# One centred-only tile instead of two at the entry of a mixer-and-MLP kernel, w2 in one load, and a new instruction order

## The chip, the cores and the metric

The kernel runs on one core of a Trainium2 chip. The metric is the device time of one execution in microseconds. "Span" is the time from the first to the last instruction in a profiled execution; it is about 1.3 us shorter than the time of the same run.

## The reference

```python
h  = gelu(layernorm(x) @ w1)                       # x: 2048 x 512, w1: 512 x 512
# four quarters of the columns of h are shifted by +1, -1, +2, -2 tokens
x1 = x + concat(g0, g1, g2, g3) @ w2               # w2: 512 x 512
out = x1 + gelu(layernorm(x1) @ w3) @ w4           # w3: 512 x 1792, w4: 1792 x 512
```

All inputs are bf16. Tokens are worked on in 16 tiles of 128.

## The kernel before

The order of TensorE is given by hand (or by a search) in a script, and so is the order of the loads. The names used below: `ty`/`tp` is a transpose of normalised rows on TensorE, `up1` the first matmul (w1), `mix` the matmul with w2, `up2` and `down` those with w3 and w4.

Most tiles take this path at the entry: statistics, rstd, normalise to rows, transpose on TensorE into PSUM, copy back to SBUF, `up1` with the result already transposed. A tile in `NAT` takes another, and this document calls it a centred-only tile. Its rows are only centred, so its transpose needs the mean but not rstd; its first matmul makes rows, and rstd is applied as the scale of the gelu. The price is a return transpose (`th`) of the gelu's result and one more copy.

```python
GROUPS = {1: (1, 1, 1, 1, 1, 1, 2, 2, 2, 2, 2), 2: (2, 2, 4, 4, 4)}   # tiles per up1 / up2 group
STAT_ACT = (1, 6, 8, 9, 12, 21, 22, 23, 27, 28, 29)                   # statistics on ScalarE, others on VectorE
NAT = (0, 1)
SPLIT = (0,)                                                          # tile 0 works in two halves of w1
LOADS = """
x0 w1a w1b x4-5 w2b tp2 x3 w2a x6-7 w3b x8 w3a x1@act x9 x2@act x11 tp16 w4a x10 tp11 w4b tp9 x12-14 x15
"""
SCRIPT = """
warm:8 sa:0 sb:0 ty:1 ra:0 rb:0 up1:1 ty:2 th:0-1 up1:2 mix:0 ty:4 ty:3 mix:1 ...
"""
# ... cut ...
def ln(layer, t):                       # cut to its order
    # bn_stats, bn_aggr (or two passes on ScalarE) -> mean, variance
    pg.add("pool", f"rstd{q}", lambda e: e.tensor_tensor(col(rstd), var, neghalf[:], ALU.pow), ...)
    # normalise: centred-only tiles do not read rstd
# ... cut ...
def warm_pe(n):                         # dummy matmuls ahead of the first useful work
    def f(e):
        for _ in range(n):
            ins = e.matmul(o_ps[:, b, :], zeros[:, 0:P], zeros[:], start=True, stop=True)
        return ins
# ... cut ...
pg.order()                              # places all operations; pg.seq is the order that is emitted
emit(nc, es, pg)
```

Each engine executes its own list in order. `x1@act` means that the load is issued from ScalarE's queue; all other loads are issued by SyncE.

Of the kernel before, what the change touches and what calls it, by code (L numbers as in the profile page):

```python
# [6 lines left out]
P = 128  # L7
ACT_F = mybir.ActivationFunctionType
# [17 lines left out]
class Program:  # L26
# [2 lines left out]

    HOP = {"pe": 200.0, "dve": 155.0, "act": 220.0, "pool": 120.0, "sp": 70.0}  # L30
    LOOK = {"dve": 300.0, "act": 300.0}
    DUE = 252723.0
    BEGIN = {"sp": 30.0, "act": 150.0, "pe": 400.0, "dve": 150.0, "pool": 450.0}
    ENTRY = 1900.0
    COLD, RESTART = 4300.0, 800.0
# [219 lines left out]
        self.seq = out  # L255
        return out

GROUPS = {1: (1, 1, 1, 1, 1, 1, 2, 2, 2, 2, 2), 2: (2, 2, 4, 4, 4)}
NORM = {4: "act", 5: "act", 6: "act", 10: "act", 11: "pool", 12: "pool", 13: "act", 15: "act", 18: "pool", 20: "pool", 21: "pool", 22: "pool", 24: "act", 28: "act", 30: "pool"}
EVAC = {1: "both", 2: "dve", 3: "dve", 7: "both", 9: "dve", 10: "both", 11: "both", 13: "both", 16: "dve", 17: "both", 19: "both", 20: "dve", 22: "both", 23: "dve", 24: "dve", 25: "dve", 28: "dve", 31: "dve"}  # L260
STAT_ACT = (1, 6, 8, 9, 12, 21, 22, 23, 27, 28, 29)
TAIL = (256, 128, 128)
NMR = {0: "pool", 1: "pool", 3: "pool", 5: "pool", 7: "pool", 9: "pool", 10: "pool", 12: "pool", 13: "pool", 14: "pool", 17: "pool", 18: "pool", 19: "pool", 21: "pool", 22: "pool", 23: "pool", 27: "pool", 30: "pool"}
NAT = (0, 1)
SPLIT = (0,)
HEV = {2: "dve", 5: "dve", 6: "dve"}
BIAS = {}
LOADS = """
x0 w1a w1b x4-5 w2b tp2 x3 w2a x6-7 w3b x8 w3a x1@act x9 x2@act x11 tp16 w4a x10 tp11 w4b tp9 x12-14 x15
"""  # L270
SCRIPT = """
warm:8 sa:0 sb:0 ty:1 ra:0 rb:0 up1:1 ty:2 th:0-1 up1:2 mix:0 ty:4 ty:3 mix:1 up1:3 ty:5 up1:4 mix:2 up1:5
mix:3 ty:17 mix:4 up2:0 up1:6 up2:1 mix:6 down:1 mix:5 up1:7-8 mix:8 mix:7 up1:9 mix:10 down:0 down:2 mix:9
up1:10 mix:12 mix:11 up2:2 mix:13 down:3 down:6 mix:14 up2:3 mix:15 down:4-5 down:7 down:11 down:9-10 up2:4
down:8 down:12 down:14 down:13 down:15
"""

def bass_standalone__mixer_s_mlp__prompt_kernel(nc, x, w1, w2, w3, w4, out):
    B, S, D = x.shape
    F = w3.shape[1]  # L280
    assert B == 1 and D == 4 * P and S % 512 == 0 and F % (2 * P) == 0 and S >= 1024
    NT, DC, FC = S // P, D // P, F // P
# [10 lines left out]
    with ExitStack() as es:  # L293
        sb = lambda name, shape, dt: es.enter_context(nc.sbuf_tensor(name, shape, dt))
        x_sb = sb("x_sb", [P, NT, D], BF16)
        x1_sb = sb("x1_sb", [P, NT, D], BF16)
        xnT = sb("xnT", [P, DC, S], BF16)
        hT = sb("hT", [P, DC, HTW], BF16)
        h2T = sb("h2T", [P, FC, S], BF16)
        w1_sb = sb("w1_sb", [P, DC, D], BF16)  # L300
# [3 lines left out]
        ident = sb("ident", [P, P], BF16)  # L304
# [26 lines left out]
        def pair_rv(p, v):  # L331
            return [(("y", p, 0), v), (("y", p, 1), v)]
# [180 lines left out]
        def mm_up_rows(t):  # L513
            p, v = next_pair()
            k = NAT.index(t)

            def part(c0, c1):
                def f(e):
                    for dc in range(c0, c1):
                        ins = e.matmul(y_ps[:, p, 0:D], xnT[:, dc, P * t : P * (t + 1)], w1_sb[:, dc, :],  # L520
                                       start=(dc == 0), stop=(dc == DC - 1))
                    return ins

                return f

            if t in SPLIT:
                for hh in (0, 1):
                    cs = range(2 * hh, 2 * hh + 2)
                    pg.add("pe", f"rows{t}_{hh}", part(2 * hh, 2 * hh + 2),
                           reads=[(("w1", c), 0) for c in cs] + [(("xT", t, c), 1) for c in cs],  # L530
                           writes=[pair_rv(p, v)[hh]], dur=2 * 215.8)
                    if hh == 0:
                        yield
            else:
                pg.add("pe", f"rows{t}", part(0, DC),
                       reads=[(("w1", c), 0) for c in range(DC)] + [(("xT", t, c), 1) for c in range(DC)],
                       writes=pair_rv(p, v), dur=DC * 215.8)
            pg.add("act", f"gelur{t}",
                   lambda e: e.activation(hn[:, k, :], y_ps[:, p, 0:D], ACT_F.Gelu_apprx_tanh,  # L539
                                          scale=rstd[:, t : t + 1]),  # L540
                   reads=pair_rv(p, v) + [(("rstd", t), 0), (("warm",), 1)], writes=[(("hn", t), 0)], dur=50 + D * 0.833)
            yield

        def h_transpose(t, pair):
            g = group_of[1, t]
            how = HEV.get(t, "act")
            k = NAT.index(t)
            if pair:
                b, v = next_pair()
                res, dst = pair_rv(b, v), y_bf[:, b, 0:D]  # L550
            else:
                b, v = next_bank()
                res, dst = [(("o", b), v)], o_bf[:, b, 0:D]

            def f(e):
                for c in range(DC):
                    ins = e.transpose(dst[:, P * c : P * (c + 1)], hn[:, k, P * c : P * (c + 1)], ident[:])  # L557
                return ins

            pg.add("pe", f"th{t}", f, reads=[(("hn", t), 0), (("ident",), 1)], writes=res, dur=225)  # L560
            to, frm = hT[:, :, 2 + P * t : 2 + P * (t + 1)], dst.rearrange("p (c s) -> p c s", s=P)
            pg.add(how, f"evh{t}",
                   (lambda e: e.activation(to, frm, ACT_F.Copy)) if how == "act" else
                   (lambda e: e.tensor_copy(to, frm)),
                   reads=res, writes=[(("h", j, g), 0) for j in range(DC)],
                   dur=(60 + 0.82 * D) if how == "act" else (75 + 0.51 * D))


        def mm_up(layer, g):
            t0, n = groups[layer][g]  # L570
# [34 lines left out]
        def run(gen):  # L605
            for _ in gen:
                pass
# [82 lines left out]
        for step in SCRIPT.split():  # L690
            kind, n = step.split(":")
            a, _, b = n.partition("-")
            steps += [(kind, n) for n in (range(int(a), int(b or a) + 1) if kind != "warm" else [int(n)])]
        steps = [s for s in steps if s[0] not in ("th", "tz") or s[1] in NAT]
        pe_tp = {n for kind, n in steps if kind in ("tp", "ty", "sa")}
        queues = {"sp": [], "act": []}
        for i, item in enumerate(LOADS.split()):
# [10 lines left out]
        for kind, n in steps:  # L708
            if kind == "warm":
                warm_pe(n)  # L710
            elif kind in ("sa", "ra"):
                halves[kind[0], n] = pe_transpose(n, n, True) if kind == "sa" else mm_up_rows(n)
                next(halves[kind[0], n])
            elif kind in ("sb", "rb"):
                next(halves[kind[0], n])
            elif kind in ("tp", "ty"):
                run(pe_transpose(n % NT, n, kind == "ty"))
            elif kind in ("th", "tz"):
                h_transpose(n, kind == "tz")
            elif kind == "mix":  # L720
                mm_mix(n)
            elif kind == "down":
                mm_down(n)
            else:
                for _ in mm_up(int(kind[2]), n):
                    pass
# [103 lines left out]
```

## Time and profile before

| | before |
|---|---|
| median of 3 runs | 135.56 us (135.43 to 135.89) |
| span of the profiled run (the slowest of the three, 135.89 us) | 134.6 us |
| TensorE busy | 130.6 us, 97% |
| first useful matmul / last one ends | 5.01 / 132.73 us |

The page's head shows the busy times; TensorE (PE) is the limit:

```profile
span 134.6 us, 2013 instructions
PE 130.6 (97%) x780; PEld 72.7 (54%) x792; DVE 52.1 (39%) x140; ACT 58.5 (44%) x90; POOL 25.9 (19%) x59
```

The timeline of TensorE at the entry has the columns start, length, engine, line, operation, output and inputs, count, and in brackets the idle time just before and what ended it. L679 is the dummies, L482 transposes, L520 the rows of centred-only tiles, L557 their return transposes, L586 `up1`:

```profile
3.18 1.06 PE L679 MATMUL o_ps<-zeros 128*128 128x512 bf16 x2
4.03 1.01 PE L482 MATMUL y_ps<-ident,xn_buf 128*128 128x128 bf16 x8
5.01 0.59 PE L520 MATMUL y_ps<-w_sb,xnT 128*128 128x512 bf16 x2
6.04 1.47 PE L520 MATMUL y_ps<-w_sb,xnT 128*128 128x512 bf16 x6 [0.44 <-DMA w_sb<-in_w_dram]
7.35 0.39 PE L482 MATMUL y_ps<-ident,xn_buf 128*128 128x128 bf16 x4
7.57 0.39 PE L557 MATMUL o_ps<-ident,hn 128*128 128x128 bf16 x4
8.35 0.40 PE L557 MATMUL o_ps<-ident,hn 128*128 128x128 bf16 x4 [0.39 <-ACT hn L539]
```

There are two waits. The second half of w1 landed at 6.00 us and is used from 6.04, and the return transpose of tile 1 waits for its gelu until 8.35. After about 9.6 us the stream has no gap worth the name.

The table of windows gives, for the first 6 us, the length, the busy time of PE, PEld, DVE, ACT and POOL, the granted clock, the DMA share and the rate in GB/s.

```profile
0.00:6.00 6.00, 4.97 (x18) 2.06 (x18) 3.22 (x11) 3.80 (x9) 2.11 (x14) 1.00 0.77 242
```

### The profile page before, as it was taken

Reading aid. Unit: us, or ns where it says so; the run is one execution under the profiler, and the core shown is the slowest. Engines: PE = TensorE matmul, PEld = TensorE weight load, DVE = VectorE, ACT = ScalarE, POOL = GpSimd, SP = SyncE. Lnnn points to the kernel's source line nnn. Section 1 sums busy time; section 2 is a strip of 40 time slices with the busy share of each in tenths; the row PEclk is TensorE's granted clock in tenths of the full one; section 3 lists DMA queues with packets and bytes.
Section 4 is the critical chain, followed back from the end, with each engine's and each line's share of the span. In section 5 each row is a group of like instructions: output and inputs, shape, how many; then the busy total and the mean of one; then the engine's idle time right before and its main releaser. Section 6 shows DMA issues by size and latency. Waiting matters only on the chain.

```text
span 134.6 us, 2013 instructions
## 1 busy us (share of the span) xinstructions
PE 130.6 (97%) x780; PEld 72.7 (54%) x792; DVE 52.1 (39%) x140; ACT 58.5 (44%) x90; POOL 25.9 (19%) x59
## 2 busy tenths in 40 slices
PE   8889999999999999999999999999999999999994
PEld 3467688886586446444444444444444444444463
DVE  3779999403947627700053500062222200012222
ACT  6598995768484402775530366500000155520000
POOL 2533467600865301200010310010000000000000
DMA  6999398599056532111003110003111100001112
GB/s 198 298 381 380 80 294 161 98 271 271 0 117 82 118 78 78 39 39 39 5 0 78 39 39 0 0 0 85 39 39 65 52 0 0 0 5 39 39 39 78
DMA packets 21897, 12.32 MB, mean 92 GB/s; under 512 B 14464, under 2 KB 21376, under 8 KB 21888
## 3 DMA queue, kind: packets, MB, share of 16 engines
q1 hardware_dynamic: 21168, 11.80, 32.9%
q10 hardware_dynamic: 720, 0.39, 1.0%
q8 instruction: 6, 0.10, 0.3%
q14 instruction: 3, 0.02, 0.0%
HBM read 6.82 MB, written 2.10 MB: 66 GB/s over the span
## 4 chain that ended last, share of the span: by engine, by line
PE 93%; DMA 4%; issue 1%; SPq 1%; ACT 1%; DVE 0%; ACTq 0%
PE y_ps L586 45%; PE o_ps L655 36%; PE o_ps L626 10%; DMA w_sb<-in_w_dram 4%; PE y_ps L520 1%; PE y_ps L482 1%; ACT hn L539 1%; SPq L372 0%; PE o_ps L557 0%; SPq L365 0%; DVE o_sb L663 0%; ACTq L779 0%; SPq L815 0%
## 5 line engine op out<-in xcount | busy, mean ns | idle before, releaser
L586 PE MATMUL y_ps<-xnT,w_sb 128*128 128x256 bf16 (+2 forms) x421 | 62.4, 306 | 0.2
L586 PEld LDWEIGHTS y_ps<-xnT,w_sb 128*128 128x128 bf16 x424 | 39.0, 98 | 23.4 <-DVE xnT L490 0.3
L655 PE MATMUL o_ps<-w_sb,h2T 128*128 128x512 bf16 (+2 forms) x247 | 49.0, 355 | 0.3
L601 ACT ACTIVATE h2T<-y_ps 128x1024 bf16<-128x1024 f32 (+1 forms) x29 | 28.6, 994 | 42.6 <-PE y_ps L586 42.6
L655 PEld LDWEIGHTS o_ps<-w_sb,h2T 128*128 128x128 bf16 x252 | 23.6, 98 | 25.2
L663 DVE TENSOR_TENSOR o_sb<-o_ps,x_sb 128x512 bf16<-128x512 f32 (+2 forms) x18 | 11.4, 633 | 40.0 <-PE o_ps L655 39.8
L416 POOL TENSOR_TENSOR rstd<-mv,neghalf 128x1 f32<-128x1 f32 x21 | 11.7, 555 | 42.8 <-DVE mv L411 38.7
L626 PE MATMUL o_ps<-w_sb,hT 128*128 128x512 bf16 x60 | 15.2, 379 | 0.3
L409 DVE BATCH_NORM_STATS2 st<-x_sb 128x6 f32<-128x512 bf16 x21 | 14.2, 676 | 2.1 <-DMA x_sb<-in_x_dram 1.8
L637 DVE TENSOR_TENSOR x_sb<-o_ps,x_sb 128x512 bf16<-128x512 f32 x10 | 6.9, 687 | 12.7 <-PE o_ps L626 12.7
L633 DVE SCALAR_TENSOR_TENSOR x_sb<-o_ps,x_sb 128x512 bf16<-128x512 f32 x6 | 4.1, 690 | 16.8 <-PE o_ps L626 16.7
L601 ACT ACTIVATE hT<-y_ps 128x1024 bf16<-128x1024 f32 (+1 forms) x9 | 7.4, 827 | 6.3 <-PE y_ps L586 6.2
L416 POOL TENSOR_TENSOR rstd<-vpe,neghalf 128x1 f32<-128x1 f32 x11 | 6.0, 551 | 18.8 <-DVE vpe L405 18.7
L626 PEld LDWEIGHTS o_ps<-w_sb,hT 128*128 128x128 bf16 x64 | 6.0, 98 | 5.5
L437 DVE TENSOR_SCALAR xn_buf<-x_sb,mv,rstd 128x512 bf16<-128x512 bf16 x15 | 7.0, 469 | 4.9 <-POOL rstd L416 4.6
L446 ACT ACTIVATE xn_buf<-x_sb,nmr,rstd 128x512 bf16<-128x512 bf16 x8 | 6.5, 813 | 5.1 <-DVE nmr L442 3.2
L393 ACT ACTIVATE junk<-x_sb 128x512 bf16<-128x512 bf16 x11 | 6.9, 624 | 2.7 <-DVE x_sb L633 2.7
L449 POOL TENSOR_SCALAR xn_buf<-x_sb,rstd,nmr 128x512 bf16<-128x512 bf16 x7 | 5.4, 768 | 0.8 <-DVE nmr L442 0.4
L679 PE MATMUL o_ps<-zeros 128*128 128x512 bf16 x8 | 3.6, 631 | 0.6 <-POOLq L815 0.6
L411 DVE BATCH_NORM_AGGREGATE mv<-st 128x2 f32<-128x9 f32 x21 | 4.0, 191 | 0.2
L388 ACT ACTIVATE junk<-x_sb 128x512 bf16<-128x512 bf16 x5 | 3.1, 625 | 0.2 <-DMA x_sb<-in_x_dram 0.2
L482 PEld LDWEIGHTS y_ps<-ident,xn_buf 128*128 128x128 bf16 x28 | 2.3, 111 | 1.3 <-issue 0.5
(35 smaller groups left out, 30.5 us busy)
## 6 DMA issues: line engine op xcount, KB each, us to landing
w_sb<-in_w_dram SPq DMA_DIRECT2D x4, 896.0 KB, 6.8
out_dram<-o_sb SPq DMA_DIRECT2D x15, 128.0 KB, 1.7
w_sb<-in_w_dram SPq DMA_DIRECT2D x4, 256.0 KB, 5.2
x_sb<-in_x_dram SPq DMA_DIRECT2D x7, 128.0 KB, 5.2
x_sb<-in_x_dram SPq DMA_DIRECT2D x2, 256.0 KB, 5.5
xnT<-xn_buf SPq DMA_TRANSPOSE x25, 2.5
x_sb<-in_x_dram SPq DMA_DIRECT2D x1, 384.0 KB, 6.0
x_sb<-in_x_dram ACTq DMA_DIRECT2D x2, 128.0 KB, 3.0
```

Of the source, the lines that this page charges most:

```text
L393: (lambda d: (lambda e: e.activation(d, src, ACT_F.Square, accum_out=sums[:, q, 1:2])))(junk[:, b, :]),
L409: pg.add("dve", f"bnst{q}", lambda e: e.bn_stats(st9[:, q, 0:6], src), reads=rs, writes=[(("st", q), 0)], dur=605)
L416: lambda e: e.tensor_tensor(col(rstd), var, neghalf[:], ALU.pow),
L437: lambda e: e.tensor_scalar(dst, src, mv[:, q, 0:1], rstd[:, q : q + 1], ALU.subtract, ALU.mult),
L446: f = lambda e: e.activation(dst, src, ACT_F.Identity, bias=nmr[:, q : q + 1], scale=rstd[:, q : q + 1])
L449: f = lambda e: e.tensor_scalar(dst, src, rstd[:, q : q + 1], nmr[:, q : q + 1], ALU.mult, ALU.add)
L586: ins = e.matmul(y_ps[:, p, W * i : W * (i + 1)], wsb[:, dc, P * fc : P * (fc + 1)], src[:, dc, P * t0 : P * t0 + W], start=(dc == 0), sto ...
L601: (lambda d, s: (lambda e: e.activation(d, s, ACT_F.Gelu_apprx_tanh)))(dst, ysrc),
L626: ins = e.matmul(dst, hT[:, j, c0 : c0 + P], w2_sb[:, j, :], start=(j == 0), stop=(j == DC - 1))
L637: f = lambda e: e.tensor_tensor(x1_sb[:, t, :], dst, x_sb[:, t, :], ALU.add)
L655: ins = e.matmul(dst, h2T[:, fc, P * t : P * (t + 1)], w4_sb[:, fc, cs], start=(fc == 0), stop=(fc == FC - 1))
L663: (lambda d, c: (lambda e: e.tensor_tensor(o_sb[:, oi, c], d, x1_sb[:, t, c], ALU.add)))(dst, cs),
```

## The change

The intent is to give up one of the two centred-only tiles, and with it one return transpose and its wait, to load w2 in one piece, and to take script, load order and engine choices from a search that averages over random late landings of loads and DMA transposes. The diff, cut to its core:

```diff
-GROUPS = {1: (1, 1, 1, 1, 1, 1, 2, 2, 2, 2, 2), 2: (2, 2, 4, 4, 4)}
+GROUPS = {1: (1, 1, 1, 1, 2, 1, 4, 2, 1, 2), 2: (2, 4, 4, 4, 2)}
-STAT_ACT = (1, 6, 8, 9, 12, 21, 22, 23, 27, 28, 29)
+STAT_ACT = (0, 4, 8, 11, 15, 17, 18, 19, 20, 21, 25, 26, 27, 28, 29, 30, 31)
-NAT = (0, 1)
+NAT = (0,)
-HEV = {2: "dve", 5: "dve", 6: "dve"}
+HEV = {0: "dve", 2: "dve"}
 LOADS = """
-x0 w1a w1b x4-5 w2b tp2 x3 w2a x6-7 w3b x8 w3a x1@act x9 x2@act x11 tp16 w4a x10 tp11 w4b tp9 x12-14 x15
+x1 x2 tp16 w1a w1b x4 x3 w2 x5 x6-7 x9-10 x0@act tp17 x11 w3a w3b x8 w4b w4a tp9 x12-13 x14-15
 """
 SCRIPT = """
-warm:8 sa:0 sb:0 ty:1 ra:0 rb:0 up1:1 ty:2 th:0-1 up1:2 mix:0 ty:4 ty:3 mix:1 ...
+warm:10 sa:0 sb:0 ty:1 ra:0 rb:0 ty:2 up1:1 th:0 up1:2 mix:0 ty:3 mix:1 ty:4-5 ...
 """
 # cut: DUE, NORM, EVAC, NMR; a rewrite of the return transpose that can split in halves (unused here: CSPLIT = ())
```

With `NAT = (0,)`, `up1:1` is tile 1 on the ordinary path. Counted over the whole script, TensorE does nine four-part transposes either way (seven and two return transposes before, eight and one after). `HEV` names the tiles whose return transpose is copied by VectorE instead of ScalarE, so tile 0's copy moves to VectorE.

More of the change, by code (lines that the diff above doesn't have):

```diff
@@ L31 @@
     LOOK = {"dve": 300.0, "act": 300.0}
-    DUE = 252723.0
+    DUE = 385824.0
     BEGIN = {"sp": 30.0, "act": 150.0, "pe": 400.0, "dve": 150.0, "pool": 450.0}
@@ L256, in place @@
         return out
-GROUPS = {1: (1, 1, 1, 1, 1, 1, 2, 2, 2, 2, 2), 2: (2, 2, 4, 4, 4)}
-NORM = {4: "act", 5: "act", 6: "act", 10: "act", 11: "pool", 12: "pool", 13: "act", 15: "act", 18: "pool", 20: "pool", 21: "pool", 22: "pool", 24: "act", 28: "act", 30: "pool"}
-EVAC = {1: "both", 2: "dve", 3: "dve", 7: "both", 9: "dve", 10: "both", 11: "both", 13: "both", 16: "dve", 17: "both", 19: "both", 20: "dve", 22: "both", 23: "dve", 24: "dve", 25: "dve", 28: "dve", 31: "dve"}
-STAT_ACT = (1, 6, 8, 9, 12, 21, 22, 23, 27, 28, 29)
+GROUPS = {1: (1, 1, 1, 1, 2, 1, 4, 2, 1, 2), 2: (2, 4, 4, 4, 2)}
@@ L262 @@
+NORM = {4: "act", 6: "pool", 8: "pool", 9: "pool", 10: "pool", 12: "act", 14: "pool", 15: "pool", 19: "pool", 20: "pool", 22: "act", 23: "act", 24: "act", 25: "act", 27: "pool", 28: "act", 31: "act"}
+EVAC = {1: "both", 2: "dve", 3: "both", 4: "both", 5: "dve", 6: "dve", 8: "both", 11: "dve", 16: "both", 17: "dve", 18: "dve", 20: "dve", 21: "both", 22: "dve", 29: "dve", 30: "dve", 31: "dve"}
+STAT_ACT = (0, 4, 8, 11, 15, 17, 18, 19, 20, 21, 25, 26, 27, 28, 29, 30, 31)
 TAIL = (256, 128, 128)
-NMR = {0: "pool", 1: "pool", 3: "pool", 5: "pool", 7: "pool", 9: "pool", 10: "pool", 12: "pool", 13: "pool", 14: "pool", 17: "pool", 18: "pool", 19: "pool", 21: "pool", 22: "pool", 23: "pool", 27: "pool", 30: "pool"}
@@ L264 @@
-NAT = (0, 1)
+NMR = {1: "pool", 3: "pool", 5: "pool", 10: "pool", 11: "pool", 12: "pool", 13: "pool", 15: "pool", 17: "pool", 20: "pool", 21: "pool", 25: "pool", 26: "pool", 27: "pool", 28: "pool", 30: "pool", 31: "pool"}
+NAT = (0,)
 SPLIT = (0,)
-HEV = {2: "dve", 5: "dve", 6: "dve"}
+CSPLIT = ()
+HEV = {0: "dve", 2: "dve"}
 BIAS = {}
 LOADS = """
-x0 w1a w1b x4-5 w2b tp2 x3 w2a x6-7 w3b x8 w3a x1@act x9 x2@act x11 tp16 w4a x10 tp11 w4b tp9 x12-14 x15
+x1 x2 tp16 w1a w1b x4 x3 w2 x5 x6-7 x9-10 x0@act tp17 x11 w3a w3b x8 w4b w4a tp9 x12-13 x14-15
@@ L270 @@
 """
 SCRIPT = """
-warm:8 sa:0 sb:0 ty:1 ra:0 rb:0 up1:1 ty:2 th:0-1 up1:2 mix:0 ty:4 ty:3 mix:1 up1:3 ty:5 up1:4 mix:2 up1:5
-mix:3 ty:17 mix:4 up2:0 up1:6 up2:1 mix:6 down:1 mix:5 up1:7-8 mix:8 mix:7 up1:9 mix:10 down:0 down:2 mix:9
-up1:10 mix:12 mix:11 up2:2 mix:13 down:3 down:6 mix:14 up2:3 mix:15 down:4-5 down:7 down:11 down:9-10 up2:4
-down:8 down:12 down:14 down:13 down:15
+warm:10 sa:0 sb:0 ty:1 ra:0 rb:0 ty:2 up1:1 th:0 up1:2 mix:0 ty:3 mix:1 ty:4-5 up1:3-4 mix:2 ty:16-17 mix:3
+up2:0 mix:4 up1:5 down:0-1 mix:5 up1:6-7 mix:7-8 up1:9 mix:9-10 up1:8 mix:6 mix:15 up2:1 mix:11-12 up2:2
@@ L276 @@
+mix:14 down:4 down:2 down:6 mix:13 up2:4 down:3 down:8 down:5 up2:3 down:7 down:12 down:11 down:10 down:9
+down:14 down:13 down:15
 """
@@ L524, in part, with f @@
                 return f
+            if t in CSPLIT:
+                H = D // 2
+                for hh in (0, 1):
+                    cs = slice(H * hh, H * (hh + 1))
+                    def f(e, hh=hh, cs=cs):
+                        for dc in range(DC):
+                            ins = e.matmul(y_ps[:, p, 512 * hh : 512 * hh + H], xnT[:, dc, P * t : P * (t + 1)],
+                                           w1_sb[:, dc, cs], start=(dc == 0), stop=(dc == DC - 1))
+                        return ins
+                    pg.add("pe", f"rows{t}_{hh}", f,
+                           reads=[(("w1", c), 0) for c in range(DC)] + [(("xT", t, c), 1) for c in range(DC)],
+                           writes=[pair_rv(p, v)[hh]], dur=DC * 109.2)
+                    pg.add("act", f"gelur{t}_{hh}",
+                           (lambda a, b: (lambda e: e.activation(a, b, ACT_F.Gelu_apprx_tanh,
+                                                                 scale=rstd[:, t : t + 1])))(
+                               hn[:, k, cs], y_ps[:, p, 512 * hh : 512 * hh + H]),
+                           reads=[pair_rv(p, v)[hh], (("rstd", t), 0), (("warm",), 1)], writes=[(("hn", t, hh), 0)],
+                           dur=50 + H * 0.833)
+                    yield
+                return
             if t in SPLIT:
@@ L540, in mm_up_rows, with h_transpose @@
                                           scale=rstd[:, t : t + 1]),
-                   reads=pair_rv(p, v) + [(("rstd", t), 0), (("warm",), 1)], writes=[(("hn", t), 0)], dur=50 + D * 0.833)
+                   reads=pair_rv(p, v) + [(("rstd", t), 0), (("warm",), 1)],
+                   writes=[(("hn", t, hh), 0) for hh in (0, 1)], dur=50 + D * 0.833)
             yield
-        def h_transpose(t, pair):
+        def h_transpose(t):
             g = group_of[1, t]
@@ L547, in h_transpose @@
             k = NAT.index(t)
-            if pair:
+            if t in CSPLIT:
                 b, v = next_pair()
-                res, dst = pair_rv(b, v), y_bf[:, b, 0:D]
+                steps = [(2 * hh, 2 * hh + 2, [pair_rv(b, v)[hh]], f"_{hh}") for hh in (0, 1)]
+                dst = y_bf[:, b, :].rearrange("p (k x) -> p k x", k=2)[:, :, 0 : D // 2]
+                chunk = lambda c: dst[:, c // 2, P * (c % 2) : P * (c % 2 + 1)]
+                part = lambda c0, c1: dst[:, c0 // 2, :].rearrange("p (c s) -> p c s", s=P)
@@ L551, in h_transpose @@
             else:
                 b, v = next_bank()
-                res, dst = [(("o", b), v)], o_bf[:, b, 0:D]
-            def f(e):
-                for c in range(DC):
-                    ins = e.transpose(dst[:, P * c : P * (c + 1)], hn[:, k, P * c : P * (c + 1)], ident[:])
-                return ins
-            pg.add("pe", f"th{t}", f, reads=[(("hn", t), 0), (("ident",), 1)], writes=res, dur=225)
-            to, frm = hT[:, :, 2 + P * t : 2 + P * (t + 1)], dst.rearrange("p (c s) -> p c s", s=P)
@@ L562, in h_transpose @@
-            pg.add(how, f"evh{t}",
-                   (lambda e: e.activation(to, frm, ACT_F.Copy)) if how == "act" else
-                   (lambda e: e.tensor_copy(to, frm)),
-                   reads=res, writes=[(("h", j, g), 0) for j in range(DC)],
-                   dur=(60 + 0.82 * D) if how == "act" else (75 + 0.51 * D))
+                steps = [(0, DC, [(("o", b), v)], "")]
+                dst = o_bf[:, b, 0:D]
+                chunk = lambda c: dst[:, P * c : P * (c + 1)]
+                part = lambda c0, c1: dst.rearrange("p (c s) -> p c s", s=P)
@@ new lines, in h_transpose, with f @@
+            for c0, c1, res, tag in steps:
+                def f(e, c0=c0, c1=c1):
+                    for c in range(c0, c1):
+                        ins = e.transpose(chunk(c), hn[:, k, P * c : P * (c + 1)], ident[:])
+                    return ins
+                n = c1 - c0
+                pg.add("pe", f"th{t}{tag}", f,
+                       reads=[(("hn", t, hh), 0) for hh in range(c0 // 2, c1 // 2)] + [(("ident",), 1)],
+                       writes=res, dur=56 * n if n < DC else 225)
+                to, frm = hT[:, c0:c1, 2 + P * t : 2 + P * (t + 1)], part(c0, c1)
+                pg.add(how, f"evh{t}{tag}",
+                       (lambda a, b: (lambda e: e.activation(a, b, ACT_F.Copy)) if how == "act" else
+                        (lambda e: e.tensor_copy(a, b)))(to, frm),
+                       reads=res, writes=[(("h", j, g), 0) for j in range(c0, c1)],
+                       dur=(60 + 0.82 * n * P) if how == "act" else (75 + 0.51 * n * P))
+                yield
@@ L693, in bass_standalone__mixer_s_mlp__prompt_kernel @@
             steps += [(kind, n) for n in (range(int(a), int(b or a) + 1) if kind != "warm" else [int(n)])]
-        steps = [s for s in steps if s[0] not in ("th", "tz") or s[1] in NAT]
+        steps = [s for s in steps if s[0] != "th" or s[1] in NAT]
         pe_tp = {n for kind, n in steps if kind in ("tp", "ty", "sa")}
@@ L710, in bass_standalone__mixer_s_mlp__prompt_kernel @@
                 warm_pe(n)
-            elif kind in ("sa", "ra"):
-                halves[kind[0], n] = pe_transpose(n, n, True) if kind == "sa" else mm_up_rows(n)
+            elif kind in ("sa", "ra", "ta"):
+                halves[kind[0], n] = {"s": lambda n: pe_transpose(n, n, True), "r": mm_up_rows,
+                                      "t": h_transpose}[kind[0]](n)
                 next(halves[kind[0], n])
-            elif kind in ("sb", "rb"):
+            elif kind in ("sb", "rb", "tb"):
                 next(halves[kind[0], n])
@@ L717, in bass_standalone__mixer_s_mlp__prompt_kernel @@
                 run(pe_transpose(n % NT, n, kind == "ty"))
-            elif kind in ("th", "tz"):
-                h_transpose(n, kind == "tz")
+            elif kind == "th":
+                run(h_transpose(n))
             elif kind == "mix":
```

## The prediction

> **What bounds the kernel now.** TensorE. On the page PE is busy 130.6 of 134.6 us (97%), and the chain of waits is 93% PE, 4% the load of w1. The timeline puts the first useful matmul (first half of tile 0) at 5.01 us, the second half of w1 at 6.04 and the end of the last matmul at 132.73: a stream of 127.7 us.
>
> Its work, from start-to-start spacings in the timeline (55.7 ns for 128 columns, 109.3 for 256, 215.8 for 512): up1 14.0, up2 48.5, mix 13.8, down 48.4, seven four-part transposes 1.5; 126.3 us. So about 1.4 us is idle: 0.44 waiting for w1's second half, some 0.6 between 7.97 and 8.59, where the two natural-layout tiles' return transposes wait for their gelus, 0.1 before the first mix, 0.3 over the remaining 124 us. The Trainium skill, "TensorE: Matmul & The Clock Gate", section "Back-to-back issue gap", gives N/2.4 GHz + 2.5 ns; the trace agrees (215.8 ns at N=512), so there is no slack inside the stream.
>
> **What the change does.** Almost nothing to the amount of PE work. One natural-layout tile fewer takes away a return transpose (0.22 us), but layer 2's tile 0 moves from a DMA transpose to PE (0.22): nine either way. Group widths change, but twice 16 matmuls of 128 (0.89 us) equal 16 of 256 (1.75) to 0.03 us. Up2, mix, down and tail are equal. ScalarE gets six more statistics tiles (0.62 + 0.19 us each, and more for layer 1), but is 44% busy.
>
> Only order can gain:
> - w1 behind x tiles: they were on the other queue before, so bytes ahead of each half are the same (0.65 and 0.91 MB, DMA share near 1 from 1.5 us in the table of windows). I expect w1 as before, 5.0 and 6.0 us, or up to 0.3 later (issue is 0.45 later).
> - After 6.04: half of tile 0, transpose of 2, up1 of tile 1 (0.89), then the return transpose. Tile 0's gelu (0.69 us) hides behind tile 1's matmuls: -0.5 to -0.6. Against it: tile 2's normalised rows are wanted near 6.5 rather than 7.35, and that normalise ended at 6.55: +0.1 to +0.3.
> - w2 in one load: all of it behind 1.7 MB; at the traced 0.33 to 0.41 MB per us and some 1.5 us to landing, near 8.3 us, wanted near 8.7. Tight.
> - The first up2 group starts near 15.9 us rather than 17.4, and needs all of w3, the last of 4.3 MB: landing 14.8 to 15.2 (estimate from the windows). Tight. w4 ahead of all DMA transposes leaves tile 6's 2 to 3 us.
>
> The search averaging over late landings pays for slack against such waits, not for a shorter undisturbed run.
>
> **Prediction.** 135.2 us, 134.5 to 136.3. Under 134.1 needs an earlier w1. Faster by over 2%: 0.01; within 2%: 0.95; slower by over 2%: 0.04.
>
> **What would show it.** PE busy stays 130 to 131 us, matmuls 780 +/- 10; the return transpose's wait for gelu goes; w1's second half starts the stream at 6.0 to 6.3; from there to the end is 0.2 to 0.7 us shorter. Idle pieces over 0.3 us at mix 0, up2 group 0 or up1 of tile 6 would show late loads instead.
>
> **What would make it wrong.** w1 over 0.5 us late because x precedes it; w3 a wait of 1 us or more; DMA transposes held behind w4 and starving up1 of tiles 6 to 10; ScalarE late with a normalise. Each makes it slower, none by itself over 2%.

## More of the kernel before

The state of every run quoted here is fast, with a granted TensorE clock of 1.0 in the records.

The program is a list of operations, each with what it reads and writes. A placing routine inside the kernel orders them per engine from estimated durations; semaphores follow from that order.

## The result, and the profile after

| | before | after |
|---|---|---|
| median of 4 runs | 135.71 us (135.43 to 135.89) | 135.75 us (135.71 to 135.79) |
| span of the profiled run | 134.6 us | 134.4 us |
| second half of w1 used from | 6.04 us | 5.65 us |
| mix 0 starts | about 9.5 us | 9.00 us |

The ratio is 1.0005, 95% interval 0.9984 to 1.0025. A ratio here is the mean time of one kernel's fast runs over that of the other's of the same rounds, so it is not quite the ratio of the medians quoted. The start of mix 0 before is worked out: the trace lacks the record of its first matmul, and the second is at 9.74, 0.22 us later.

The page after:

```profile
span 134.4 us, 2046 instructions
PE 131.4 (98%) x790; PEld 71.5 (53%) x790; DVE 50.4 (38%) x156; ACT 60.9 (45%) x100; POOL 27.3 (20%) x61
```

The same stretch of TensorE's timeline after (L712 dummies, L483 transposes, L521 rows of tile 0, L587 its return transpose, L619 `up1`, L659 mix):

```profile
3.18 1.14 PE L712 MATMUL o_ps<-zeros 128*128 128x512 bf16 x4
4.22 0.83 PE L483 MATMUL y_ps<-ident,xn_buf 128*128 128x128 bf16 x8
5.06 1.20 PE L521 MATMUL y_ps<-w_sb,xnT 128*128 128x512 bf16 x4
6.09 0.39 PE L483 MATMUL y_ps<-ident,xn_buf 128*128 128x128 bf16 x4
6.32 1.06 PE L619 MATMUL y_ps<-xnT,w_sb 128*128 128x128 bf16 x16
7.28 0.40 PE L587 MATMUL o_ps<-ident,hn 128*128 128x128 bf16 x4
8.09 1.07 PE L619 MATMUL y_ps<-xnT,w_sb 128*128 128x128 bf16 x16 [0.42 <-DVE xnT L491]
9.00 0.38 PE L659 MATMUL o_ps<-w_sb,hT 128*128 128x512 bf16 x1
```

The wait for the gelu is gone, as intended: the return transpose at 7.28 follows `up1` of tile 1 but for some 0.07 us (the gelu ended at 7.22), where it was 0.56 before. But a hole of the same size stands right behind it. The four parts of the return transpose take 0.22 us, so `up1` of tile 2 could have started at 7.50; it starts at 8.09, 0.59 us later. VectorE's timeline shows why:

```profile
5.69 0.28 DVE L491 COPY xnT<-y_ps 128x256 bf16<-128x256 bf16 x1
7.02 0.69 DVE L410 BATCH_NORM_STATS2 st<-x_sb 128x6 f32<-128x512 bf16 x1 [1.04 <-DMA x_sb<-in_x_dram]
7.63 0.41 DVE L491 COPY xnT<-y_ps 128x512 bf16<-128x512 bf16 x1
```

The copy at 7.63 carries the transpose of tile 2, made by 6.5. In VectorE's list it stands behind the statistics of tile 3, and those wait until 7.02 for x3 to land. VectorE is idle for 1.04 us, from 6.5 us on with work ready behind. Not all of the 0.59 us could have been won in this trace: w2 landed at 8.65 us, so mix 0 could have started 0.3 us earlier at most.

The table of windows after, for the first 6 us:

```profile
0.00:6.00 6.00, 5.31 (x22) 2.04 (x23) 3.40 (x12) 3.84 (x10) 2.62 (x15) 1.00 0.72 213
```

### The profile page after: what moved, and what is told of

Its sections match the earlier page's. It is cut to its first block, busy times and chain, and to the rows that moved or that the text cites. A ratio compares the mean times of both kernels' runs of the same rounds, so it can differ in the third digit from the quotient of the medians.

```text
span 134.4 us, 2046 instructions
## 1 busy us (share of the span) xinstructions
PE 131.4 (98%) x790; PEld 71.5 (53%) x790; DVE 50.4 (38%) x156; ACT 60.9 (45%) x100; POOL 27.3 (20%) x61
## 4 chain that ended last, share of the span: by engine, by line
PE 93%; DMA 3%; DVE 1%; SPq 0%; issue 0%
PE y_ps L619 45%; PE o_ps L688 36%; PE o_ps L659 10%; DMA x_sb<-in_x_dram 3%; PE y_ps L483 1%; DVE st L410 1%; SPq L366 0%; DVE xnT L491 0%; DVE o_sb L696 0%
## 5 line engine op out<-in xcount | busy, mean ns | idle before, releaser
L619 PE MATMUL y_ps<-xnT,w_sb 128*128 128x512 bf16 (+2 forms) x424 | 63.6, 309 | 0.4 <-DVE xnT L491 0.4
L619 PEld LDWEIGHTS y_ps<-xnT,w_sb 128*128 128x128 bf16 x424 | 38.3, 98 | 25.4 <-DVE xnT L491 0.6
L394 ACT ACTIVATE junk<-x_sb 128x512 bf16<-128x512 bf16 x17 | 10.6, 621 | 14.5 <-DVE x_sb L666 14.4
L417 POOL TENSOR_TENSOR rstd<-vpe,neghalf 128x1 f32<-128x1 f32 x17 | 9.3, 554 | 34.3 <-DVE vpe L406 34.3
L659 PE MATMUL o_ps<-w_sb,hT 128*128 128x512 bf16 x64 | 15.8, 379 | 0.0
L666 DVE SCALAR_TENSOR_TENSOR x_sb<-o_ps,x_sb 128x512 bf16<-128x512 f32 x12 | 8.2, 682 | 19.9 <-PE o_ps L659 19.8
L417 POOL TENSOR_TENSOR rstd<-mv,neghalf 128x1 f32<-128x1 f32 x15 | 8.2, 551 | 18.9 <-DVE mv L412 18.9
L410 DVE BATCH_NORM_STATS2 st<-x_sb 128x6 f32<-128x512 bf16 x15 | 10.1, 680 | 3.1 <-DMA x_sb<-in_x_dram 2.9
L634 ACT ACTIVATE hT<-y_ps 128x512 bf16<-128x512 f32 (+1 forms) x10 | 8.1, 808 | 6.8 <-PE y_ps L619 6.8
L659 PEld LDWEIGHTS o_ps<-w_sb,hT 128*128 128x128 bf16 x64 | 6.1, 98 | 5.8
L712 PE MATMUL o_ps<-zeros 128*128 128x512 bf16 x10 | 3.7, 541 | 0.6 <-POOLq L849 0.6
L406 DVE SCALAR_TENSOR_TENSOR vpe<-sums,mv 128x1 f32<-128x1 f32 x17 | 2.8, 169 | 3.1 <-ACT junk L394 2.8
L670 DVE TENSOR_TENSOR x_sb<-o_ps,x_sb 128x512 bf16<-128x512 f32 x4 | 2.8, 692 | 2.8 <-PE o_ps L659 2.7
L389 ACT ACTIVATE junk<-x_sb 128x512 bf16<-128x512 bf16 x5 | 3.1, 627 | 1.1 <-DMA x_sb<-in_x_dram 1.1
L402 DVE TENSOR_SCALAR mv<-mv 128x1 f32<-128x1 f32 x17 | 3.3, 203 | 0.3
```

The lines of the kernel that those rows point to most:

```text
L394: (lambda d: (lambda e: e.activation(d, src, ACT_F.Square, accum_out=sums[:, q, 1:2])))(junk[:, b, :]),
L410: pg.add("dve", f"bnst{q}", lambda e: e.bn_stats(st9[:, q, 0:6], src), reads=rs, writes=[(("st", q), 0)], dur=605)
L619: ins = e.matmul(y_ps[:, p, W * i : W * (i + 1)], wsb[:, dc, P * fc : P * (fc + 1)], src[:, dc, P * t0 : P * t0 + W], start=(dc == 0), sto ...
L634: (lambda d, s: (lambda e: e.activation(d, s, ACT_F.Gelu_apprx_tanh)))(dst, ysrc),
L659: ins = e.matmul(dst, hT[:, j, c0 : c0 + P], w2_sb[:, j, :], start=(j == 0), stop=(j == DC - 1))
L666: f = lambda e: e.scalar_tensor_tensor(x1_sb[:, t, :], dst, 1.0, x_sb[:, t, :], ALU.mult, ALU.add, accum_out=sums[:, NT + t, 0:1])
```

## The experiments

Three theories took shape in turn. Theory A: the gain was given back by VectorE's order (tile 3's statistics ahead of tile 2's copy). Theory W: the two added dummies cost time in the runs in which the clock switches late. (By the switch I mean the moment at which the spacing of equal matmuls on TensorE halves: in the trace after, the dummies start 0.43 us apart at first and 0.22 us apart from 3.50 us on.) Theory L: the new order of loads moves fewer bytes early. Where an experiment keeps the placed order and moves single operations, it does so after `pg.order()`:

```python
seq = pg.seq
def behind(name, anchor):
    op = next(o for o in seq if o.name == name)
    seq.remove(op)
    seq.insert(1 + next(i for i, o in enumerate(seq) if o.name == anchor), op)
```

All twelve gave correct results (the labels e5 and e7 do not occur on record). They ran in three calls of four, each call on one chip with 11 runs of the kernel before between them.

| run | median us (range) | ratio to before (95%) | span |
|---|---|---|---|
| before 1 / 2 / 3 | 135.63 / 135.47 / 135.43 | | |
| e0_before_again | 135.12 (134.96 to 135.99) | 0.9976 (0.9943 to 1.0010) | 133.9 |
| e1_copy_first | 136.08 (135.57 to 136.31) | 1.0029 (1.0005 to 1.0054) | 134.8 |
| e2_copies_first | 136.48 (136.28 to 136.78) | 1.0070 (1.0047 to 1.0094) | 134.9 |
| e3_x3_late | 137.07 (136.49 to 137.27) | 1.0100 (1.0070 to 1.0129) | 135.8 |
| e8_after_again | 135.81 (135.54 to 136.22) | 1.0030 (1.0002 to 1.0058) | 134.3 |
| e9_after_warm8 | 135.75 (135.29 to 136.39) | 1.0026 (0.9994 to 1.0057) | 135.0 |
| e10_warm8_copy_first | 135.89 (135.54 to 136.59) | 1.0037 (1.0007 to 1.0066) | 134.4 |
| e11_before_warm10 | 135.89 (135.24 to 136.46) | 1.0027 (0.9995 to 1.0060) | 135.1 |
| e12_after_x2_act | 135.76 (135.44 to 135.82) | 1.0019 (0.9993 to 1.0044) | 134.1 |
| e13_x2_act_warm8_copy | 135.88 (135.66 to 136.23) | 1.0034 (1.0007 to 1.0060) | 134.6 |
| e4_before_one | 136.19 (135.85 to 137.86) | 1.0071 (1.0022 to 1.0120) | 136.3 |
| e6_after_w2_halves | 135.70 (135.26 to 135.93) | 1.0015 (0.9987 to 1.0043) | 134.6 |

### e0_before_again: the kernel before, unchanged

> The kernel before, unchanged, as a null test and a second trace of it. Both theories: ratio 1.000 within 0.3%. What it tells: whether the landing of the second half of w1 (6.04 us in the first trace of before, 5.65 in the trace after) moves from run to run. If that landing is a matter of chance, this trace shows it elsewhere between 5.5 and 6.1 us and the span moves with it, between 134.2 and 134.6; if it is fixed by the order of loads, it is at 6.0 again within 0.1.

Measured: a span of 133.9 us, below the expected range. TensorE's timeline has all eight matmuls of tiles 0 and 1 in one piece, with no wait for w1:

```profile
5.00 1.89 PE L520 MATMUL y_ps<-w_sb,xnT 128*128 128x512 bf16 x8
7.73 0.40 PE L557 MATMUL o_ps<-ident,hn 128*128 128x128 bf16 x4 [0.39 <-ACT hn L539]
```

So the landing of w1's second half is a matter of the run: it came at 6.00 us in the first trace and at 4.67 here (5.46 and 5.60 in the two later traces with the old load order), and it cost 0.44 us of waiting in the first trace and nothing here, and the gelu wait was the same in both. The two spans differ by 0.7 us, and mix 0 (worked out as above) started at 8.90 here against 9.5. The kernel before spreads over 1 us on one chip (134.93 to 135.98). A difference of 0.3 us between kernels needs many runs, and single traces are for seeing mechanisms, not for ranking.

### e1_copy_first: tile 3's statistics behind tile 2's copy

```diff
+behind("bnst3", "ev2")
```

> The kernel after, with VectorE's statistics of tile 3 issued behind its copy of tile 2's transpose instead of ahead of it; nothing else differs. Theory A (the 0.59 us before up1 of tile 2 is VectorE's own order: it sits on tile 3's statistics until x3 lands at 7.0, with a copy behind it that was ready at 6.5): up1 of tile 2 starts at 7.5 instead of 8.09, at once behind the return transpose. Since VectorE is over 90% busy from 7 to 16 us, I expect 0.2 to 0.45 us of it in the span (133.95 to 134.2) and the rest as a new wait before mix 0 or at the transposes of tiles 4 and 5; ratio to before 0.996 to 0.999. Theory B (the gap comes from something that the copy itself waits for, such as late tile 2 rows): the start of up1 of tile 2 stays at 8.0 to 8.1 and the span at 134.4. Theory C (the whole of the 0.59 is lost anyway to the next limit): up1 of tile 2 at 7.5 but the span 134.35 to 134.5.

```profile
4.88 1.06 PE L483 MATMUL y_ps<-ident,xn_buf 128*128 128x128 bf16 x8
5.87 1.14 PE L521 MATMUL y_ps<-w_sb,xnT 128*128 128x512 bf16 x4
7.97 0.39 PE L587 MATMUL o_ps<-ident,hn 128*128 128x128 bf16 x4
8.19 1.06 PE L619 MATMUL y_ps<-xnT,w_sb 128*128 128x128 bf16 x16
```

The hole is gone: `up1` of tile 2 starts 0.22 us after the return transpose, that is at once. From the first useful matmul to the end of the span it took 128.9 us (134.8 - 5.87) against 129.3 after (134.4 - 5.06): 0.4 us less. That does not show a gain, though: e8_after_again below, with the old order of VectorE and dummies as late as here, takes 128.4 us (134.3 - 5.86). And the kernel was not faster, for the first useful matmul came at 5.87 instead of 5.06. Nothing in the edit touches that. What differs is the dummies: their starts are 0.43 us apart to the last one, where after the last ones follow at half that, so the first transposes began at 4.88 instead of 4.22. Here theory W began. Only half of the expectation was met; the time went the wrong way.

### e2_copies_first: tile 0's copy out of PSUM moved forward as well

```diff
+behind("bnst3", "ev2"); behind("th0", "bnst3"); behind("evh0", "th0")
```

> As the run before this, and tile 0's copy back out of PSUM also ahead of tile 3's aggregate on VectorE, so that mix 0 can start by 8.4. Theory A: mix 0 starts at 8.4 to 8.5 (9.00 in the trace after), span 0.0 to 0.2 us under that of the run with the one copy moved. If VectorE's load is the next limit, the two runs agree within 0.1 us and the wait is seen at tiles 4 and 5.

The median was 0.4 us above the run with the one copy moved, a miss. The first useful matmul came at 5.37, and mix 0 at about 8.9 us (9.10 for its second matmul, the first lacks a record), not at 8.4. VectorE then waited 0.17 us for the return transpose with tile 3's aggregate behind it, the normalise of tiles 3 and 4 came later, and TensorE waited 0.30 us for tile 4's rows at 11.36. Moving one operation forward in a full list moves others back: in the trace after, VectorE is busy 6.7 of the 7 us from 7 to 14 us by the table of windows.

### e3_x3_late: double the suspected wait

```diff
+behind("dma_x3", "dma_w2")
```

> The kernel after, with the load of x3 issued behind the 512 KB load of w2, so that it lands later by about 512 KB at 0.35 MB per us, 1.4 us (8.2 to 8.6 us). Theory A: VectorE sits idle until then, up1 of tile 2 starts 1.0 to 1.6 us later (9.1 to 9.7), and the span grows by 0.9 to 1.6 us (135.3 to 136.0), ratio 1.007 to 1.012. Theory B: up1 of tile 2 stays at 8.0 to 8.1, and only tile 3's own transpose, later in the stream, may wait: span up by 0 to 0.7.

VectorE and TensorE in this trace:

```profile
8.43 0.69 DVE L410 BATCH_NORM_STATS2 st<-x_sb 128x6 f32<-128x512 bf16 x1 [2.51 <-DMA x_sb<-in_x_dram]
9.04 0.41 DVE L491 COPY xnT<-y_ps 128x512 bf16<-128x512 bf16 x1
9.50 1.07 PE L619 MATMUL y_ps<-xnT,w_sb 128*128 128x128 bf16 x16 [1.48 <-DVE xnT L491]
```

x3 came 1.41 us later (8.43 for 7.02) and `up1` of tile 2 started 1.41 us later (9.50 for 8.09). The ratio is 1.010, as expected. Theory A's mechanism is shown: the load of a tile that TensorE does not need yet holds up one that it does, through the order of VectorE. Theory B, which had the copy itself late, falls.

### e8_after_again: the kernel after, unchanged

> The kernel after, unchanged, as the yardstick of this chip. In the traces so far its ten dummy matmuls ended at 4.31, 5.09 (copy moved), 4.5 (two copies moved) and 4.95 us (x3 late), though nothing ahead of them differs: the spacing of the ninth and tenth is 0.43 us at the slow clock and 0.22 at the full one, and the moment of the switch moves from run to run. If so this run has a wider spread than the first four of it (135.71 to 135.79): 135.5 to 136.4, ratio 1.000 to 1.005.

```profile
3.17 1.91 PE L712 MATMUL o_ps<-zeros 128*128 128x512 bf16 x4
4.87 1.06 PE L483 MATMUL y_ps<-ident,xn_buf 128*128 128x128 bf16 x8
5.86 1.03 PE L521 MATMUL y_ps<-w_sb,xnT 128*128 128x512 bf16 x4
8.06 1.06 PE L619 MATMUL y_ps<-xnT,w_sb 128*128 128x128 bf16 x16
8.96 0.59 PE L659 MATMUL o_ps<-w_sb,hT 128*128 128x512 bf16 x2
```

This is the same program as in the first trace after, where the dummies end at 4.32 (3.18 + 1.14); here they end at 5.08 (3.17 + 1.91). The first useful matmul comes 0.80 us later, yet mix 0 starts at 8.96 instead of 9.00 and the span is 134.3 instead of 134.4. Tile 2's copy was done at 7.57, and `up1` of tile 2 waited for nothing. Two things differ: TensorE is late, and x3 landed at 6.44 instead of 7.00. So in these two traces the two costs, dummies (0.80) and copy (0.59), do not add: each has one of them and reaches mix 0 at nearly the same time. The hole before `up1` of tile 2 is itself a matter of the run. Of the four traces that keep this order of VectorE and its place for x3, only the first has it; x3 landed at 6.44 here, at 6.33 in e9 and at 6.26 in e6. The first four runs after lay within 0.08 us of each other, the six here within 0.68.

On this chip the kernel after was 0.3% slower than before (the interval excludes 1.000, barely).

### e9_after_warm8: eight dummies

```diff
-for _ in range(n):
+for _ in range(n - 2):
```

> The kernel after with eight dummy matmuls instead of ten, all else in the same order. Theory W (the two added dummies stand ahead of the first transposes and cost up to 0.85 us in runs where the clock switches late): first transpose at 4.0 to 4.25 us in its trace, first useful matmul at 5.0 to 5.2, and 0.1 to 0.5 us faster than the kernel after of the same rounds, with a smaller spread. Rival (the extra dummies pay for themselves, by bringing the full clock to the transposes, or the w1 load sets the start anyway): within 0.1 us of the kernel after, or slower.

```profile
4.15 0.83 PE L483 MATMUL y_ps<-ident,xn_buf 128*128 128x128 bf16 x8 [0.15 <-DVE xn_buf L428]
5.01 1.29 PE L521 MATMUL y_ps<-w_sb,xnT 128*128 128x512 bf16 x4
7.36 0.40 PE L587 MATMUL o_ps<-ident,hn 128*128 128x128 bf16 x4
7.60 1.06 PE L619 MATMUL y_ps<-xnT,w_sb 128*128 128x128 bf16 x16
9.47 0.38 PE L659 MATMUL o_ps<-w_sb,hT 128*128 128x512 bf16 x1 [0.82 <-DMA w_sb<-in_w_dram]
```

Mechanism right, gain nil. The first transposes and the first useful matmul came where theory W put them, and the eight parts took the same 0.83 us as behind ten dummies in the trace after. In both the clock had switched before them (where it had not, they took 1.06 us in e8), so the rival, that more dummies speed up the transposes, is not tested by this trace. `up1` of tile 2 follows the return transpose at once although VectorE's order is unchanged: x3 came early enough. Then mix 0 waited 0.82 us for w2, whose single load took 6.4 us from its issue at 2.97. A third limit had been standing there: in the other traces of the new load order the same load landed 5.2 to 5.7 us after issue. The times were no better than with ten dummies (135.75 against 135.81) and no steadier.

### e10_warm8_copy_first: both

```diff
-for _ in range(n):
+for _ in range(n - 2):
+behind("bnst3", "ev2")
```

> Eight dummies, and tile 3's statistics behind the copy of tile 2. Theories A and W together: their gains add, for they lie at different places: 0.2 to 0.45 us under the run with eight dummies alone; 0.4 to 0.8 under the kernel after; ratio to before 0.994 to 0.999. If A is empty (the run with the one copy moved was slower for the reason that A is wrong and not by the dummies), it is no faster than eight dummies alone.

A miss: 135.89. In its trace `up1` of tile 2 began at 7.38, 0.71 us ahead of the kernel after, and mix 0 at 8.71, only 0.29 ahead: it waited 0.28 us for w2. From mix 0 to the end it took 125.7 us against 125.4 after, because the transposes of tile 4 then waited for its rows, which ScalarE's normalise delivers from VectorE's chain. Nothing was left.

### e11_before_warm10: the dummies put on the kernel before

```diff
-for _ in range(n):
+for _ in range(n + 2):
```

> The kernel before with ten dummy matmuls instead of eight: the suspected cost put on the other kernel. Theory W: slower than before by 0.1 to 0.5 us, ratio 1.001 to 1.004, first transpose at 4.4 to 4.9 instead of 4.03. Rival: ratio 0.999 to 1.001.

The first useful matmul came at 5.86 instead of 5.01, the first transpose at 4.88 instead of 4.03, and the span of this trace was 135.1. The ratio 1.0027 lies where theory W put it, but the interval reaches 0.9995, so the average cost is likely, not shown. What the trace shows is the delay in one run.

### e12_after_x2_act: one x load back on ScalarE's queue

```diff
-x1 x2 tp16 w1a w1b x4 x3 w2 x5 x6-7 x9-10 x0@act tp17 x11 ...
+x1 tp16 w1a w1b x4 x3 w2 x5 x6-7 x9-10 x0@act x2@act tp17 x11 ...
+behind("bnst2", "bnag1")      # keeps VectorE's order as it was after
```

> The kernel after with one thing moved: the load of x2 goes out on ScalarE's queue behind x0, as two of the first three x loads did in the kernel before; all engines keep the order of the kernel after. In the first 6 us the seven traces with the new load order moved 206 to 222 GB/s, the three with the old one 242 to 273. Theory L (with two x loads on SyncE's queue ahead of w1, each following load is issued some 0.45 us later and the early loads are slower as a whole): first 6 us at 235 to 270 GB/s; w2 lands 0.3 to 0.6 us earlier (by 8.4 at the latest, 8.4 to 9.4 so far), w1's second half before 5.6; time 0.1 to 0.4 us under the kernel after of the second job (135.81), ratio to before 0.999 to 1.002, held back by the ten dummies. Rival (the slower rate comes of the sizes or the order of the loads behind, not of the queue): 205 to 225 GB/s, no gain.

The window line of the first 6 us, and VectorE where the cost came up:

```profile
0.00:6.00 6.00, 5.17 (x20) 1.96 (x21) 2.91 (x10) 3.65 (x9) 2.13 (x15) 1.00 0.79 258
3.84 0.69 DVE L410 BATCH_NORM_STATS2 st<-x_sb 128x6 f32<-128x512 bf16 x1 [0.51 <-DMA x_sb<-in_x_dram]
4.45 0.46 DVE L428 TENSOR_SCALAR xn_buf<-x_sb,mv 128x256 bf16<-128x256 bf16 x2
```

The rate rose to 258 GB/s, as theory L asked (265 in the next experiment); w1's second half landed at 4.72 us and w2 at 8.14, as it asked too. x2 itself landed later, though, at 3.81 us (3.02 in the trace after), and VectorE had its statistics ahead of tile 0's centring. The first transpose moved to 4.87 and the first useful matmul to 5.70. The span is the shortest of the family, 134.1, but the profiled run was the fastest of its six, and the median (135.76) is the same. It is theory A's fault once more, one tile earlier: by keeping VectorE's order fixed I had built it in.

### e13_x2_act_warm8_copy: all three eased

The edits of e12 (without the pinned order of tile 2's statistics), e9 and e1 together.

> All three limits of the entry eased at once: x2 on ScalarE's queue, eight dummies, tile 3's statistics behind the copy. If the entry of the kernel after is a race of three limits that fall within half a microsecond of each other (dummies, copy, w2), so that easing one or two shows nothing, easing three must show: 0.4 to 0.9 us under the kernel after, ratio to before 0.993 to 0.999, mix 0 at 8.2 to 8.6 us. If it is no faster than 135.6, the theory of three limits is wrong or a fourth lies as close.

```profile
4.16 0.58 PE L483 MATMUL y_ps<-ident,xn_buf 128*128 128x128 bf16 x4
5.18 0.61 PE L483 MATMUL y_ps<-ident,xn_buf 128*128 128x128 bf16 x4 [0.44 <-DVE xn_buf L438]
5.58 1.25 PE L521 MATMUL y_ps<-w_sb,xnT 128*128 128x512 bf16 x4
```

A miss again: 135.88. The placing routine put tile 2's statistics ahead of tile 1's normalise, and x2 came late, so tile 1's transpose, which stands ahead of tile 0's matmuls in the script, waited until 5.18. Mix 0 began at 8.90. By the words of the expectation the theory of three limits is too small: a fourth, x2 on VectorE's list, lay as close.

### e4_before_one: the named part alone

```diff
-NAT = (0, 1)
+NAT = (0,)
```

> The kernel before with one natural-layout tile instead of two, alone (the placement moves a few VectorE and ScalarE instructions with it). The prediction's step: tile 0's gelu hides behind tile 1's matmuls, the 0.6 us wait of the second return transpose goes. If it holds here: 0.2 to 0.5 us faster, ratio 0.996 to 0.999. If the copy of tile 2, which now stands behind tile 3's statistics and so behind x3, takes it back: ratio 0.999 to 1.003 and a wait for that copy of 0.3 us or more before up1 of tile 2.

```profile
4.75 0.40 PE L482 MATMUL y_ps<-ident,xn_buf 128*128 128x128 bf16 x2 [0.18 <-DVE xn_buf L427]
5.66 0.61 PE L482 MATMUL y_ps<-ident,xn_buf 128*128 128x128 bf16 x4 [0.52 <-DVE xn_buf L437]
6.06 1.91 PE L520 MATMUL y_ps<-w_sb,xnT 128*128 128x512 bf16 x4
7.77 1.78 PE L586 MATMUL y_ps<-xnT,w_sb 128*128 128x128 bf16 x16
10.30 1.07 PE L586 MATMUL y_ps<-xnT,w_sb 128*128 128x128 bf16 x16 [0.30 <-DVE xnT L490]
```

Alone this part is a loss of 0.7% on average, with a wait for tile 2's copy as the second guess said. But two larger parts are things that I had not listed. As a centred-only tile, tile 1 could be transposed without rstd. Now its transpose waits for its normalise, which waits for two passes on ScalarE, two small VectorE steps and rstd and stands behind tile 2's statistics: 5.66 us instead of about 4.5, and the first useful matmul at 6.06 instead of 5.01. The full change avoids that by putting x1 first on SyncE's queue and its statistics on VectorE. Two of the six runs took 137.64 and 137.86; the profiled one is the first of them, and its trace shows the other part: the clock switched only at 9.3 us. The four row matmuls of tile 0 start 0.43 us apart (0.22 at the full clock) and the sixteen of tile 1's `up1` 0.107 apart (0.056), which makes an estimated 1.7 us, as much as the gap to the four other runs (135.85 to 136.21, 136.04 on average). Whether the run of 137.86 was late in the same way isn't shown, nor what delayed the switch. The four others alone are 0.4% slower than before.

### e6_after_w2_halves: w2 in two loads

```diff
-x1 x2 tp16 w1a w1b x4 x3 w2 x5 ...
+x1 x2 tp16 w1a w1b x4 x3 w2b w2a x5 ...
```

> The kernel after with w2 in two halves again, alone. Mix 0 needs all of w2 either way, so one load or two should make no difference: ratio to before within 0.2% of the kernel after of the second job (1.003), that is 1.001 to 1.005. If one load of 512 KB lands late as such, halves gain 0.1 to 0.3 us and the later half lands before 8.4.

135.70, ratio 1.0015, inside the expected range: one load or two makes no difference that shows. Mix 0 began at 8.95 with no wait. One other thing came up in this trace: `up1` of tile 6 started at 23.55, some 0.3 us after mix 4 was through (22.36 plus 4 x 0.216), held by a DMA transpose:

```profile
22.36 1.03 PE L659 MATMUL o_ps<-w_sb,hT 128*128 128x512 bf16 x4
23.55 1.05 PE L619 MATMUL y_ps<-xnT,w_sb 128*128 128x128 bf16 x16 [0.16 <-DMA xnT<-xn_buf]
```

That is one of the late landings that the prediction named. It was not there in the trace after, where the same group began at 23.37.

## Why the prediction was right or wrong

- **The total.** 135.2 us, range 134.5 to 136.3, within 2%: measured 135.75, inside the range. What it forecast as the likely outcome, some 0.4 us of gain, did not come; that the range held is owed to its width (1.8 us, no change included) and not to the account of the gain. The pooled runs are 135.51 us on average for 41 of before and 135.80 for 10 of after, so if anything the change costs 0.2%.
- **"PE busy stays 130 to 131 us, matmuls 780 +/- 10": near.** 131.4 us and 790. The count of matmuls did not really rise by ten: the page before has 780 matmul records for 792 weight loads, the page after 790 for 790, so twelve records are missing before and the true number fell by two (also why the busy times of the two pages compare badly). The text did not count the two dummies at all. That was an omission, not a mis-sized term: they are 0.43 us each while the clock is slow, and they precede every useful instruction of TensorE.
- **"the return transpose's wait for gelu goes": right.** By the starts of the matmuls it was 0.56 us in the first trace before, and at most 0.11 us is left in any trace of the new order (e9).
- **The step that failed** is "-0.5 to -0.6. Against it: tile 2's normalised rows are wanted near 6.5 rather than 7.35 ... +0.1 to +0.3". The gain's first half is right. The second term named the wrong operation and was too small. Tile 2's rows were in time (its transpose ran at 6.09). Their copy back was not, since it stood behind tile 3's statistics on VectorE, which sat on x3 until 7.02: 0.59 us in the trace after, as much as the gain. e3_x3_late shows the mechanism one to one. It is not what every run loses: in e8, e9 and e6 x3 landed 0.56 to 0.74 us earlier and the hole is absent. There late dummies (0.80 us, e8; alike in e6) or w2 (0.82 us, e9) took the time instead.
- **"w1's second half starts the stream at 6.0 to 6.3; from there to the end is 0.2 to 0.7 us shorter": wrong twice.** It was used from 5.65, and from there to the end of the last matmul took 126.92 us (132.57 - 5.65) against 126.69 before (132.73 - 6.04). e0_before_again shows that 6.04 was chance, so the prediction took one run's wait for the kernel's.
- **"bytes ahead of each half are the same": true of the bytes, wrong in what I drew from it.** In the first 6 us the four traces with the old load order moved 242 to 273 GB/s, the eight with the unchanged queues of the new order 206 to 222. With x2 on the other queue it was 258 and 265. w2 was foreseen "near 8.3 us ... tight"; it landed at 8.4 (e8), 8.6 (after) and 9.4 (e9). It was waited for only in runs in which everything else was early (e9, e10). w3, also called tight, landed at 15.37 in the trace after, a microsecond before the first `up2` group began at 16.40.
- **"so there is no slack inside the stream".** The spacing is as stated, 215.8 ns. The section that the prediction names gives its formula for isolated matmuls, so it is the measured spacing, and not the page, that speaks for the whole stream here.
- **"The search ... pays for slack ..., not for a shorter undisturbed run": agrees with the runs, not proved.** The 10 runs of after lie within 0.68 us, the 41 of before within 1.17 us, but those are more runs on more chips.

From mix 0 on neither kernel loses anything: span minus mix 0 is 125.1 us in the first trace of before (134.6 - 9.5) and 125.4 and 125.3 in the two of after, which has one transpose of 0.22 us more to do there. So the whole difference between these kernels is decided before 9 us, and there at least four things end within half a microsecond or so of each other: the dummies' end, tile 2's copy behind x3, w2, and tile 1's rows behind x2 (the last made late by the edits of e12 and e13 themselves). The moment of the clock's switch moves the first of them from run to run, and the landings move the others. Each was made visible in a trace by easing another. No variant was faster than before. That these limits take turns over all the runs is inferred from one trace of each kernel or variant; it is not counted.

**What stays open:** how often the clock switches late, and how often each limit is the last; the average cost of the two dummies (0.1 to 0.5 us was expected, the interval includes none); why the queue of one x load changes the rate of all early loads; what delays the switch to 9.3 us in e4_before_one; how much fewer than eight dummies would cost or gain, since no run had fewer.

## What to carry to other kernels

When a wait is removed, look at the next instruction on each engine that feeds the limiting one: in an in-order list, an operation that waits for a load blocks ready work behind it, so put statistics of a tile that nobody needs yet behind the copies that somebody does (in e1 and e10 that removed the wait, though it gained no time here). Where several limits end within the spread of the landings, easing one shows nothing, and one trace per kernel is not enough to tell: rerun the unchanged kernels first. Dummy matmuls ahead of the first useful work are not free if the time at which the clock switches varies from run to run. And look at the spacing of equal matmuls before explaining a slow run: a late switch shows there.

## What the Trainium skill lacked or had wrong

- "TensorE: Matmul & The Clock Gate", section "What's actually happening", says that the window is free-running and that the moment of the switch therefore varies by 500 ns either way. That it varies agrees with the traces: the same ten dummies let the first transpose begin at 4.22 us in one run of the same program and 4.87 in another. But it varies by more: in the trace after, the spacing is that of the full clock from 3.50 us on; in e8_after_again, the same program, it is still the slow 0.107 us for the transposes at 5.5, and in e4_before_one up to 9.3. The first dummy starts at 0.63 to 0.65 us in all of them. The page lacks the consequence for a kernel that warms up by a count of matmuls: two more dummies delayed the first useful matmul by 0.85 us in a late case (5.86 in e11_before_warm10 for 5.01 before). The advice there not to fit to a cold count holds. The record of the granted clock was no help: it reads 1.00 from the first window on, while the dummies were 0.43 us apart.
- "DMA: Bandwidth & Descriptors", section "Issuing engines are not separate DMA queues", says that issuing from several engines only saves the sequencer's issue time, usually small. Here that choice went with the rate of the first 6 us: 206 to 222 GB/s with one x load on ScalarE's queue (eight traces), 242 to 273 with two (six traces, two of them the new order with x2 moved: 258 and 265). The runs do not show whether issue time alone explains it.
- No page that I used speaks of the cost of an in-order engine list under late loads; here 1.41 us of later x3 became 1.41 us of later matmul through VectorE.
